# Attention keys transposed by DMA instead of by TensorE, with block-wide loads, a deeper MLP lag and an instruction order made from modelled times

## The chip, the cores and the metric

The kernel runs on one core of a Trainium2 chip. The metric is the device time of one execution in microseconds (us).

The engines are named as the profile names them. PE is TensorE (matmuls, and transposes done as matmuls), PEld is its weight load, DVE is VectorE, ACT is ScalarE, POOL is GpSimd. SP only issues DMAs here, on its own queue (SPq). The program fixes the order of the instructions on each engine. In the traces of this case an instruction that waits holds up those behind it on its engine (below, DVE stands 11.6 us before one instruction while others are behind it), and this whole case turns on that.

## The reference, cut to what matters

B=4 batches, H=8 heads, S=768 tokens, D=64. Keys are grouped into 24 chunks of 32. An upper bound of each query's score against a chunk comes from the chunk's elementwise minimum and maximum. Each query attends only to its six best chunks, causally. The result is fed to a two-layer ELU network, 512 to 2048 to 512.

```python
k_min = np.min(k_chunks, axis=3); k_max = np.max(k_chunks, axis=3)   # over 32 keys
ub = np.sum(np.maximum(q * k_min, q * k_max), axis=-1)               # bound of query x chunk
top_chunks = np.argsort(np.where(causal, ub, -1e9))[..., -6:]
attn = softmax(where(selected and causal, q @ k.T / 8, -1e9)) @ v    # shortened
h = x @ w_in
out = np.where(h > 0, h, np.exp(np.minimum(h, 0)) - 1) @ w_out
```

## The kernel before

The work is cut into eight blocks, one for each batch and half of the queries. In a block, for each pair of heads, K and Q are transposed on PE, the bounds are computed, chunks are selected, and scores, exponentials and PV follow. The normalised attention of a block then goes through the MLP: 64 matmuls `h_ps` (128x384) and 48 matmuls `o_ps` (128x512) for each block, so 512 and 384 in the whole run.

Attention has many small steps that wait for one another across PE, ACT and DVE. MLP matmuls have few such waits. So the kernel tells the scheduler, by priorities (`span`), to run the MLP of block i among the attention of block i+1, as filler for PE.

```python
def prep(t, hf):                              # one pair of heads
    ...
    for n in range(3):
        nc.tensor.transpose(ps[:, P * n:P * (n + 1)], k_pair[:, n], ident_f)    # psK
    nc.vector.tensor_reduce(out=kmm[:, 0, :], in_=pv, axis=AX.X, op=AOT.min)    # chunk bounds
    nc.vector.tensor_reduce(out=kmm[:, 1, :], in_=pv, axis=AX.X, op=AOT.max)
    for h in range(2):
        nc.scalar.activation(out=lhs[s][h][0:64, ts], in_=ps[64 * h:64 * h + 64, :], func=AF.Copy)
    ...                                       # rows 64 to 95 of lhs: constant mask rows
for i in range(len(blocks)):
    at = span(i, *SP_A[i])
    for t in pairs_of(blocks[i][0]):
        attend(t, blocks[i][1], ...)
    mm_h, last_e = mlp(*blocks[i], span(i + 1, *SP_M[i]))   # SP_M = [(0.0, 1.0)] * 8
    ...                                       # loads, front (prep and select) of block i + 1
```

The names in the profile: `psK`, `psQ` and `pxt` are transposes done on PE, `ub` the bounds, `sps` the scores, `pt` their exponentials, `o` the products with V, `on` the normalised attention and `xt` its transpose. `lhs` and `rhs` hold the transposed keys and queries.

In `mlp`, each `h_ps` tile goes through ACT (exp), POOL (minus one) and DVE (`gT`, the ELU). It occupies one of four PSUM buffers until the DVE step has read it.

The softmax here doesn't subtract the row's maximum and nothing guards it: scores larger than these inputs give would overflow.

## Time and profile before

| | before |
|---|---|
| median of 3 runs | 338.99 us (338.86 to 339.16) |
| span of the profiled run | 338.3 us |
| PE busy, idle | 303.8, 34.5 us |
| ACT, DVE, POOL busy | 231.4, 223.2, 98.3 us |
| DMA queue q1 (SP's: most loads of Q, K and V, transposes, stores), share of 16 engines | 32.8% |

Here are lines of the page of the kernel before: the busy time of the engines, then busy tenths in 40 equal slices of the span. PEclk is the granted TensorE clock in tenths.

```profile
PE 303.8 (90%) x2328; PEld 165.8 (49%) x2328; DVE 223.2 (66%) x690; ACT 231.4 (68%) x506; POOL 98.3 (29%) x219
...
PE   3776999998899979999989998999999998999895
...
PEclk9955799999999998999999999999999999999999
DMA  7899977542422677566232313223200111000001
```

After the fifth slice (about 42 us) PE is at nine tenths nearly everywhere, while DMA falls well below full. These are the groups of instructions that matter, with busy us, mean ns of one, and the idle time just before them with what ended most of it:

```profile
L321 PE MATMUL h_ps<-xt,w_in_sb 128*128 128x384 bf16 x512 | 107.1, 334 | 8.3 <-DMA xt<-on 4.6
L334 PE MATMUL o_ps<-w_out_sb,gT 128*128 128x512 bf16 x384 | 99.5, 379 | 0.9 <-DVE gT L328 0.8
...
L179 PE MATMUL psK<-ident_f,k_pair 128*128 128x128 f32 x96 | 20.0, 300 | 6.1 <-POOL kst_146 L138 4.1
L181 DVE TENSOR_REDUCE kmm<-psK 128x12 f32<-128x384 f32 x32 | 17.6, 550 | 6.3 <-PE psK L179 6.1
```

PE's waits in the kernel before (total us, times, longest us) are all small:

```profile
PE h_ps L321 <- DMA xt<-on: 4.6, 5, 2.3
PE psK L179 <- POOL kst_146 L138: 4.1, 1, 4.1
PE pxt L306 <- DVE on L299: 3.7, 3, 1.4
PE h_ps L321 <- DVE gT L328: 3.5, 8, 1.0
```

The windows view of the kernel before, 60 to 140 us. Columns: stretch and its length, then busy us with the count of instructions for PE, PEld, DVE, ACT and POOL, then the granted clock, the DMA share and GB/s.

```profile
60.00:80.00 20.00, 18.87 (x168) 9.70 (x166) 12.71 (x51) 17.65 (x40) 0.00 (x0) 1.00 0.48 122
80.00:100.00 20.00, 17.07 (x155) 10.03 (x155) 15.75 (x50) 18.60 (x42) 4.97 (x10) 1.00 0.33 73
100.00:120.00 20.00, 18.77 (x157) 9.48 (x156) 15.95 (x55) 12.32 (x26) 7.36 (x15) 1.00 0.44 103
120.00:140.00 20.00, 17.22 (x115) 9.52 (x113) 13.05 (x40) 13.14 (x31) 8.07 (x17) 0.91 0.69 166
```

### The profile page before, as it was taken

The numbers are of one execution on the slowest core, as the hardware profiler recorded it, in microseconds if no ns is written. First come the engines' busy times: TensorE is split into PE (matmuls) and PEld (weight loads), VectorE is DVE, ScalarE is ACT, GpSimd is POOL, SyncE is SP. The second block draws the span as 40 slices with busy tenths as digits, with TensorE's granted clock in tenths as the row PEclk, the third lists the DMA queues.
The fourth block names the chain that finished last, engine by engine and source line by source line (L and its number), as shares of the span: only waits on it lengthen the run. The fifth ranks groups of instructions, "written<-read, shape, count | busy, mean of one in ns | idle before, by whom it ended". The sixth has DMA issues, their size and how long they took to land.

```text
span 338.3 us, 6875 instructions
## 1 busy us (share of the span) xinstructions
PE 303.8 (90%) x2328; PEld 165.8 (49%) x2328; DVE 223.2 (66%) x690; ACT 231.4 (68%) x506; POOL 98.3 (29%) x219
## 2 busy tenths in 40 slices
PE   3776999998899979999989998999999998999895
PEld 2444544444454435555654455555554445545552
DVE  5888578566798673875479874866479765622640
ACT  5643585799995718976797649966797647856531
POOL 8750442000055214641153003420053004400530
PEclk9955799999999998999999999999999999999999
DMA  7899977542422677566232313223200111000001
GB/s 175 163 186 202 200 161 175 155 114 60 103 51 60 137 179 186 133 140 148 71 87 52 98 56 89 61 58 92 75 14 12 45 39 37 0 33 34 31 24 69
DMA packets 94498, 32.16 MB, mean 95 GB/s; under 512 B 87296, under 2 KB 91392, under 8 KB 94464
## 3 DMA queue, kind: packets, MB, share of 16 engines
q1 hardware_dynamic: 88640, 27.15, 32.8%
q0 software_dynamic: 4224, 4.19, 7.6%
q10 hardware_dynamic: 1600, 0.39, 0.5%
q8 instruction: 18, 0.29, 0.4%
q14 instruction: 16, 0.13, 0.1%
HBM read 27.26 MB, written 6.29 MB: 99 GB/s over the span
## 4 chain that ended last, share of the span: by engine, by line
PE 32%; DVE 24%; issue 18%; ACT 17%; POOL 5%; DMA 3%; SPq 0%; POOLq 0%; ACTq 0%
PE o_ps L334 11%; PE h_ps L321 9%; DVE gT L328 6%; ACT pt L265 5%; ACT e_sb L325 4%; PE sps L262 4%; PE ub L220 3%; POOL e_sb L326 3%; DMA xt<-on 2%; DVE kmm L181 2%; DVE kmm L182 2%; PE psK L179 1%; DVE on L299 1%; DVE ubT L223 1%; DMA v_pair<-in_v_dram 1%
## 5 line engine op out<-in xcount | busy, mean ns | idle before, releaser
L326 POOL TENSOR_SCALAR e_sb<-e_sb 128x384 f32<-128x384 f32 x128 | 65.7, 521 | 190.8 <-ACT e_sb L325 186.9
L321 PE MATMUL h_ps<-xt,w_in_sb 128*128 128x384 bf16 x512 | 107.1, 334 | 8.3 <-DMA xt<-on 4.6
L334 PE MATMUL o_ps<-w_out_sb,gT 128*128 128x512 bf16 x384 | 99.5, 379 | 0.9 <-DVE gT L328 0.8
L328 DVE SCALAR_TENSOR_TENSOR gT<-h_ps,e_sb 128x384 bf16<-128x384 f32 x128 | 69.1, 552 | 32.7 <-POOL e_sb L326 30.9
L265 ACT ACTIVATE pt<-sps 128x384 bf16<-128x384 f32 (+1 forms) x160 | 79.0, 538 | 16.6 <-PE sps L262 15.3
L325 ACT ACTIVATE e_sb<-h_ps 128x384 f32<-128x384 f32 x128 | 61.3, 502 | 30.5 <-PE h_ps L321 29.9
L321 PEld LDWEIGHTS <-w_in_sb 128*128 128x128 bf16 x512 | 49.6, 100 | 40.8 <-issue 17.2
L334 PEld LDWEIGHTS <-gT 128*128 128x128 bf16 x384 | 35.4, 97 | 36.5 <-issue 3.8
L337 ACT ACTIVATE o_sb<-o_ps 128x512 f32<-128x512 f32 x24 | 14.3, 598 | 35.4 <-PE o_ps L334 32.2
L293 PEld LDWEIGHTS <-pt 128*128 128x128 bf16 x672 | 29.2, 100 | 17.6 <-DVE pt L274 5.1
L274 DVE TENSOR_TENSOR pt<-pt,tri_196 128x512 bf16<-128x512 bf16 x32 | 14.3, 446 | 18.8 <-ACT pt L265 18.8
L179 PE MATMUL psK<-ident_f,k_pair 128*128 128x128 f32 x96 | 20.0, 300 | 6.1 <-POOL kst_146 L138 4.1
L181 DVE TENSOR_REDUCE kmm<-psK 128x12 f32<-128x384 f32 x32 | 17.6, 550 | 6.3 <-PE psK L179 6.1
L268 ACT ACTIVATE pt<-sps 128x512 bf16<-128x512 f32 x32 | 19.5, 609 | 2.6 <-PE sps L262 2.2
L199 ACT ACTIVATE QTf<-psQ 128x192 f32<-128x192 f32 (+1 forms) x32 | 13.2, 413 | 10.1 <-PE psQ L198 7.0
L198 PE MATMUL psQ<-ident_f,q_pair 128*128 128x128 f32 x96 | 18.3, 304 | 1.2 <-ACT lhs_155 L184 0.3
L202 DVE TENSOR_SCALAR Qrl<-QTf 128x192 f32<-128x192 f32 (+1 forms) x32 | 11.7, 365 | 11.5 <-ACT QTf L199 11.0
L179 PEld LDWEIGHTS psK<-ident_f,k_pair 128*128 128x128 f32 x96 | 12.0, 149 | 13.0 <-POOL kst_146 L138 4.1
L182 DVE TENSOR_REDUCE kmm<-psK 128x12 f32<-128x384 f32 x32 | 17.5, 547 | 0.0
L198 PEld LDWEIGHTS psQ<-ident_f,q_pair 128*128 128x128 f32 x96 | 11.3, 151 | 11.8 <-ACT lhs_155 L184 2.0
L280 DVE TENSOR_TENSOR pt<-pt,tri_196 128x256 bf16<-128x256 bf16 x32 | 10.6, 333 | 7.7 <-ACT pt L268 7.7
L223 DVE STREAM_TRANSPOSE ubT<-ub 128x192 f32<-128x192 f32 (+1 forms) x16 | 7.7, 480 | 11.3 <-PE ub L220 11.3
(348 smaller groups left out, 400.7 us busy)
## 6 DMA issues: line engine op xcount, KB each, us to landing
k_pair<-in_k_dram SPq DMA_DIRECT2D x64, 96.0 KB, 2.5
v_pair<-in_v_dram SPq DMA_DIRECT2D x64, 96.0 KB, 2.4
out_dram<-o_sb SPq DMA_DIRECT2D x24, 256.0 KB, 2.1
q_pair<-in_q_dram SPq DMA_DIRECT2D x60, 96.0 KB, 2.4
w_in_sb<-in_moe_w_in_dram POOLq DMA_DIRECT2D x4, 512.0 KB, 8.4
w_out_sb<-in_moe_w_out_dram POOLq DMA_DIRECT2D x4, 512.0 KB, 17.0
q_pair<-in_q_dram ACTq DMA_DIRECT2D x4, 96.0 KB, 2.9
xt<-on SPq DMA_TRANSPOSE x24, 2.4
```

What stands on the lines that cost most here:

```text
L179: nc.tensor.transpose(ps[:, P * n:P * (n + 1)], k_pair[:, n], ident_f)
L181: nc.vector.tensor_reduce(out=kmm[:, 0, :], in_=pv, axis=AX.X, op=AOT.min)
L182: nc.vector.tensor_reduce(out=kmm[:, 1, :], in_=pv, axis=AX.X, op=AOT.max)
L198: nc.tensor.transpose(ps[:, P * n:P * (n + 1)], q_pair[:, n], ident_f)
L265: nc.scalar.activation(out=pt[:, hd, 0:wtot], in_=sps[:, 0:wtot], func=AF.Exp, scale=SCALE)
L268: nc.scalar.activation(out=pt[:, :, 0:256], in_=sps[:, :].rearrange("p (h w) -> p h w", h=2), func=AF.Exp, scale=SCALE)
L293: nc.tensor.matmul(o3[:, hd, qi, :], lhsT=pt[:, hd, P * qt + off:P * qt + off + P], rhs=vexts[s][:, kb, hd, :], start=(kb == 0), stop=(kb ...
L321: mm = nc.tensor.matmul(hw, lhsT=w_in_sb[:, kk, P * fc:P * (fc + 1)], rhs=xT[NPAIR * b + kk, hf], start=(kk == 0), stop=(kk == NKK - 1))
L325: nc.scalar.activation(out=e_sb, in_=hw, func=AF.Exp)
L326: last_e = nc.gpsimd.tensor_scalar(out=e_sb, in0=e_sb, scalar1=-1.0, scalar2=1.0, op0=AOT.add, op1=AOT.mult)
L328: nc.vector.scalar_tensor_tensor(out=gT[:, fc, :], in0=hw, scalar=0.0, in1=e_sb, op0=AOT.max, op1=AOT.min)
L334: nc.tensor.matmul(o_ps, lhsT=gT[:, fc, P * tt:P * (tt + 1)], rhs=w_out_sb[:, fc, :], start=(fc == 0), stop=(fc == NFC - 1))
```

## The change

Its intent is to relieve PE. K is cast to bf16 on POOL into padded tiles that already hold the mask rows, and the DMA engines transpose them. Only block 0 keeps its K on PE. The chunk bounds come from a second copy of K, loaded chunk by chunk into 96 partitions and reduced there by DVE. Loads are block-wide, and the MLP lags two blocks more. One line asks the scheduler to order the instructions by a simulated timeline, that is, by modelled times. I call this "the modelled order". The core of the diff, with cuts marked:

```diff
-SP_A = [(0.0, 0.5)] + [(0.0, 0.9)] * 7
-SP_F = [(0.5, 1.0)] + [(0.0, 0.8)] * 7
+SP_A = (0.0, 0.9)
+SP_F = (0.0, 0.8)
+LAG = 3
 ...
+    ctx.enter_context(tc.block(schedule_with_timeline_sim=True))
 ...
+    def load_c(b, hf):                      # K again, one chunk of 32 keys in each partition
+        kc = ldpool.tile([H * HCH, CHUNK * D], F32, name="kc", bufs=1)
 ...
+    def bounds(b, hf, behind=()):
 ...
+        kv = kc[:, :].rearrange("p (w d) -> p d w", d=D)
+        for x in range(2):
+            for w, op in ((0, AOT.min), (1, AOT.max)):
+                d2 = slice(D // 2 * x, D // 2 * (x + 1))
+                red = nc.vector.tensor_reduce(out=kmm[:, w, d2], in_=kv[:, d2], axis=AX.X, op=op)
 ...
+        nc.tensor.transpose(kT[:, 0:n], kmm[...], ident_f[0:n, 0:n])
 ...
+    def keys(b, hf):
 ...
+        for n in range(3):
+            casts += [nc.gpsimd.tensor_scalar(out=kbn[hf][:, n, :, 0:D], in0=kl[:, n], ...)]
+            nc.sync.dma_start_transpose(out=lh[:, n], in_=kbn[hf][:, n].rearrange("p h d -> p (h d)"))
 ...
-    casts = vpart(0)
-    w_ins = []
-    with tc.issue_after(casts[1].ins):
-        w_ins += [load_w_in(0), load_w_in(1)]
+    vpart(0)
+    load_block(1)
 ...
+    casts = back(1, (-0.3, 0.0))            # back: bounds and keys of a block
+    with tc.issue_after(casts[WGATE].ins):
+        w_ins = [load_w_in(i) for i in range(4)]
 ...
-        mm_h, last_e = mlp(*blocks[i], span(i + 1, *SP_M[i]))
+        mm_h, last_e = mlp(*blocks[i], span(i + LAG, *SP_M))
 ...
+            back(i + 2, SP_B, [norms[j] for j in BEHIND])
```

## The prediction

> **What bounds the kernel now.** TensorE. The page gives PE 303.8 of 338.3 us busy (90%), ACT 231 (68%), DVE 223 (66%), POOL 98 (29%). After 40 us the twenty-microsecond windows leave PE idle only 0.4 to 2.9 us each, so what shortens PE's work shortens the kernel. The Trainium skill, "Perfetto Trace Analysis", section Identifying the Most-Contended Engine, warns that matmul busy time is not distance to the roofline. The trace agrees: in the pure MLP tail the chain shows 48 h_ps matmuls in 7.96 us (166 ns each) and 48 o_ps in 10.37 us (216 ns), while over the whole run the groups give 209 and 259 ns of busy time each. From such dense pieces I estimate PE's real work at about 283 us: MLP 168, scores 36, PV 20, K and Q transposes 18 each, bounds 19, pxt 3. So some 55 us of the span are start, a low granted clock (0.5 from 17 to 34 us), small waits (26 us listed for PE: xt transposes 4.6, gT 4.3, on 3.7, ...), and loss from interleaving.
>
> **Removed.** 84 of 96 K transposes on PE: 3 take 0.55 us in a dense stretch, so 15.4 us of PE (17.5 us by busy time). 56 K evictions on ACT, 0.48 us each: about 27 us. On DVE 56 reduces of 0.55 us (31 us), 56 small tensor_tensors of 0.2 us (11 us), most of the mask-row copies (about 6 us).
>
> **Added.** 28 DVE reduces of 96x1024 elements: estimated 1.1 to 1.3 us each from 384 elements in 0.55 us, 31 to 36 us, so no gain there; small copies, 3 us. DVE falls by about 10 us in all. POOL: 21 K casts of 512 columns, est. 0.7 us each from 0.52 us for 384, 15 us; it has room. 21 DMA transposes of eight 128x128 blocks: the three-block one takes 1.18 us to issue and 2.4 us to land, so est. 3 us and 4 to 5 us; SP's queue has room and they are prefetched a block ahead. Another 5.5 MB of K is read in long rows; DMA is only full before 45 us.
>
> **Moved.** MLP lags two blocks and is always ready filler, and the order is made from modelled times: xt, gT and on waits (about 12 us) should mostly vanish. But block 1's four loads (3.1 MB at about 180 GB/s, 17 us) come before or among the weights, so the first h_ps should move from 32.6 to 37-45 us, with attention of blocks 0 and 1 filling PE thinly, and perhaps a longer low-clock stretch. The tail is a long dense MLP.
>
> **Sum.** Before, at 42 us about 262 of the 283 us of work remained and took 294 us (89%). After, about 248 remain at 42 us; at 89% that is 278 us, end 320; at 93%, end 309. I take 313 us, range 301 to 327. Chances: faster by over 2% 0.90, within 2% 0.07, slower 0.03.
>
> **What would show it.** PE busy 275 to 292 us; ACT near 205; DVE 205 to 220; POOL 105 to 120; psK only 12 transposes; first h_ps at 37-45 us; busy time per h_ps matmul below 200 ns; no xt entry over 2 us in PE's waits. Wrong if: h_ps start later than 50 us; a granted clock near 0.5 beyond 45 us; PE waiting on DMA transposes (scores on lhs); DVE's 1.2 us reduces blocking gT and so PE over 8 us in all; the modelled order fitting the chip badly, with head-of-line waits on PE or SP.
>
> **What would make it wrong.** Chiefly a weak start (little PE work before weights land), or strided reduces slower than one element per cycle, making DVE the limit.

## The result, and the profile after

The kernel after took 366.12 us (median of four runs, 365.93 to 366.73), against 338.93 us for the kernel before in the same rounds. The ratio is 1.081, with a 95% interval of 1.079 to 1.083: slower, where I had given slower three chances in a hundred. All ratios here are the mean time of one kernel's runs over that of the other's runs in the same rounds, so they are not quite the ratio of the medians quoted. Executions over 1.5% slower than the fastest of the same kernel are left out of the means.

| | before | after |
|---|---|---|
| span | 338.3 | 364.1 |
| PE busy | 303.8 | 297.3 |
| PE idle (span less busy) | 34.5 | 66.8 |
| of it up to 40 us | 12.0 | 16.6 |
| 40 to 80 us | 2.4 | 18.7 |
| 80 to 200 us | 9.5 | 20.2 |
| after 200 us | 10.6 | 11.2 |
| ACT, DVE, POOL busy | 231.4, 223.2, 98.3 | 207.8, 239.9, 111.7 |
| share of DMA queue q1 | 32.8% | 60.1% |

Set beside before, the loss lies in PE standing idle between 40 and 200 us (27 us more) and a little before that. Here are the same lines of the page of the kernel after:

```profile
PE 297.3 (82%) x2235; PEld 164.8 (45%) x2251; DVE 239.9 (66%) x629; ACT 207.8 (57%) x450; POOL 111.7 (31%) x220
...
PE   4756575349676877999968999999899999998795
...
PEclk9955988559989896999996999999999999999899
DMA  8899999999899899999998470020421002010002
```

DMA is full for more than half of the span, where it had been only at the start. The groups after (the trace misses 16 of the 384 `o_ps` records, worth about 16 x 0.24 = 4 us, so PE's true busy time is up to 301 us):

```profile
L400 PE MATMUL h_ps<-xt,w_in_sb 128*128 128x384 bf16 x512 | 104.9, 342 | 20.1 <-DVE gT L407 19.5
...
L413 PE MATMUL o_ps<-w_out_sb,gT 128*128 128x512 bf16 x368 | 88.3, 385 | 1.5 <-DVE gT L407 0.5
...
L204 DVE TENSOR_REDUCE kcm<-kc 96x32 f32<-96x1024 f32 x28 | 51.5, 1888 | 14.9 <-DMA kc<-in_k_dram 11.6
```

PE's waits after:

```profile
PE h_ps L400 <- DVE gT L407: 19.5, 8, 10.0
PE pxt L382 <- DVE on L375: 7.0, 4, 5.4
...
PE sps L337 <- DMA lhs_369<-kbn_140: 4.0, 1, 4.0
```

The wait for `xt`, which the lag was to remove, is gone. In its place PE waits 19.5 us for `gT`, that is, for DVE, ten of them at once. It also waits 4.0 us for keys transposed by DMA (`lhs`), a sign that the prediction had named. The windows view after shows where (same columns as before):

```profile
60.00:80.00 20.00, 7.90 (x26) 3.18 (x27) 10.01 (x13) 6.92 (x14) 2.59 (x5) 0.51 1.13 162
80.00:100.00 20.00, 17.16 (x149) 9.39 (x149) 6.88 (x17) 9.27 (x21) 5.70 (x10) 0.98 0.97 186
100.00:120.00 20.00, 14.83 (x165) 9.22 (x166) 18.20 (x56) 13.42 (x29) 4.72 (x8) 0.91 1.15 204
120.00:140.00 20.00, 13.30 (x89) 5.87 (x87) 16.30 (x47) 14.48 (x32) 4.46 (x8) 0.88 1.08 164
```

From 60 to 80 us PE ran 26 matmuls instead of 168, at about half the clock. The Trainium skill, "TensorE: Matmul & The Clock Gate", section Part 1: The HAM clock gate, says that a PE which idles for a window of a few microseconds drops to half clock until it has been busy again. The trace agrees on the drop: PE was idle from 57.1 to 61.1 us, in the wait for `lhs`, and the granted clock fell to 0.5 at 60.3 us. It stayed there until 80.8 us, also from 62 to 68 us, where PE was busy for 4.8 of 6 us.

The causes of this stall can be followed through three timelines. Columns: start us, us, engine or queue, line, operation, output and input, count; in brackets the idle time before it and what ended that. First, the queue of SP in the kernel after:

```profile
28.95 27.19 SPq L226 DMA_TRANSPOSE lhs_369<-kbn_140  x3
56.24 5.13 SPq L109 DMA_DIRECT2D kc<-in_k_dram  x8
```

Issuing three transposes of keys holds the queue for 27 us, while the weights are being loaded. Only then can the loads of `kc` for the next block be issued. Second, DVE:

```profile
69.99 7.19 DVE L204 TENSOR_REDUCE kcm<-kc 96x32 f32<-96x1024 f32 x4 [11.61 <-DMA kc<-in_k_dram]
77.10 1.47 DVE L407 SCALAR_TENSOR_TENSOR gT<-h_ps,e_sb 128x384 bf16<-128x384 f32 x3
```

DVE stands 11.6 us at the reduces because `kc` has not landed. The reduces take 7.2 us, and only behind them in DVE's order come the `gT` steps that free PSUM. Third, PE:

```profile
77.70 1.44 PE L400 MATMUL h_ps<-xt,w_in_sb 128*128 128x384 bf16 x4 [9.99 <-DVE gT L407]
```

So one late DMA passed through DVE's order and then through PE's order, and cost PE 10 us. That explains this stall, but not yet the 27 us of the result, as the experiments show.

Why 256-byte packets were slow there can be counted in the trace. From 29 to 56 us, while the three transposes were being issued, 3767 packets of 256 bytes of SP's queue moved beside 3862 packets of 1024 bytes of the weights, about one for one. The Trainium skill, "DMA: Bandwidth & Descriptors", section Queues, rings and completion order, states that an engine takes turns between its queues packet by packet. The trace agrees in so far as the two counts are nearly equal. It does not show how many of the packets that it lists go in one turn. So the small packets got a fifth of the bytes (3767 x 256 over the sum of both).

A second difference is less visible: how evenly the MLP is spread. The table counts `h_ps` and `o_ps` matmuls started in each stretch, from the windows view of these tiles.

| us | 60-80 | 80-100 | 100-120 | 120-140 | 140-160 | 160-180 | 180-200 |
|---|---|---|---|---|---|---|---|
| before | 28 | 36 | 55 | 57 | 54 | 69 | 58 |
| after | 7 | 53 | 11 | 11 | 64 | 67 | 36 |

### The profile page after: what moved, and what is told of

Its sections match the earlier page's. It is cut to its first block, busy times and chain, and to the rows that moved or that the text cites. A ratio compares the mean times of both kernels' runs of the same rounds, so it can differ in the third digit from the quotient of the medians.

```text
span 364.1 us, 6429 instructions
## 1 busy us (share of the span) xinstructions
PE 297.3 (82%) x2235; PEld 164.8 (45%) x2251; DVE 239.9 (66%) x629; ACT 207.8 (57%) x450; POOL 111.7 (31%) x220
## 3 DMA queue, kind: packets, MB, share of 16 engines
q1 hardware_dynamic: 110480, 38.16, 60.1%
## 4 chain that ended last, share of the span: by engine, by line
PE 52%; DMA 19%; DVE 16%; ACT 4%; SPq 3%; issue 2%; POOL 2%; DVEq 0%; ACTq 0%
PE o_ps L413 20%; PE h_ps L400 17%; DVE kcm L204 7%; DMA kc<-in_k_dram 5%; DMA v_ld<-in_v_dram 5%; PE sps L337 5%; PE ub L294 4%; DMA lhs_369<-kbn_140 4%; DMA k_ld<-in_k_dram 3%; DVE gT L407 2%; SPq L102 2%; DVE on L375 1%; POOL e_sb L405 1%; ACT pt L341 1%; PE psQ L272 1%
## 5 line engine op out<-in xcount | busy, mean ns | idle before, releaser
L400 PE MATMUL h_ps<-xt,w_in_sb 128*128 128x384 bf16 x512 | 104.9, 342 | 20.1 <-DVE gT L407 19.5
L341 ACT ACTIVATE pt<-sps 128x384 bf16<-128x384 f32 (+1 forms) x160 | 81.2, 533 | 44.7 <-PE sps L337 44.1
L413 PE MATMUL o_ps<-w_out_sb,gT 128*128 128x512 bf16 x368 | 88.3, 385 | 1.5 <-DVE gT L407 0.5
L204 DVE TENSOR_REDUCE kcm<-kc 96x32 f32<-96x1024 f32 x28 | 51.5, 1888 | 14.9 <-DMA kc<-in_k_dram 11.6
L413 PEld LDWEIGHTS <-gT 128*128 128x128 bf16 x384 | 37.1, 99 | 44.0 <-issue 4.4
L369 PEld LDWEIGHTS <-pt 128*128 128x128 bf16 x672 | 31.1, 102 | 20.3 <-DVE pt L350 6.6
L272 PE MATMUL psQ<-ident_f,q_ld 128*128 128x128 f32 x96 | 19.0, 311 | 2.7 <-ACT rhs_135 L275 1.1
L224 POOL TENSOR_SCALAR kbn_140<-k_ld 128x512 bf16<-128x512 f32 x12 | 7.4, 618 | 32.4 <-DMA k_ld<-in_k_dram 26.1
L272 PEld LDWEIGHTS psQ<-ident_f,q_ld 128*128 128x128 f32 x96 | 13.1, 159 | 7.2 <-ACT rhs_135 L275 1.5
L356 DVE TENSOR_TENSOR pt<-pt,tri_154 128x256 bf16<-128x256 bf16 x32 | 10.1, 315 | 7.6 <-ACT pt L344 7.6
L188 POOL TENSOR_SCALAR vext_127<-v_ld 128x512 bf16<-128x512 f32 (+1 forms) x13 | 8.0, 619 | 19.2 <-DMA v_ld<-in_v_dram 19.2
L224 POOL TENSOR_SCALAR kbn_139<-k_ld 128x512 bf16<-128x512 f32 x9 | 5.7, 630 | 21.3 <-DMA k_ld<-in_k_dram 21.2
```

Source lines behind the costliest of these rows:

```text
L204: red = nc.vector.tensor_reduce(out=kmm[:, w, d2], in_=kv[:, d2], axis=AX.X, op=op)
L272: nc.tensor.transpose(ps[:, P * n:P * (n + 1)], ql[:, n, 2 * r:2 * r + 2], ident_f)
L341: nc.scalar.activation(out=pt[:, hd, 0:wtot], in_=sps[:, 0:wtot], func=AF.Exp, scale=SCALE)
L369: nc.tensor.matmul(o3[:, hd, qi, :], lhsT=pt[:, hd, P * qt + off:P * qt + off + P], rhs=vexts[b % 2][:, kb, 2 * r + hd, :], start=(kb == 0 ...
L400: mm = nc.tensor.matmul(hw, lhsT=w_in_sb[:, kk, P * fc:P * (fc + 1)], rhs=xT[NPAIR * b + kk, hf], start=(kk == 0), stop=(kk == NKK - 1))
L413: nc.tensor.matmul(o_ps, lhsT=gTs[fc // 4][:, fc % 4, P * tt:P * (tt + 1)], rhs=w_out_sb[:, fc, :], start=(fc == 0), stop=(fc == NFC - 1))
```

## The experiments

My first theories were these. A: the start, where block 1's loads, transposes and the weights collide. B: the new path of K itself, above all the strided reduces and their bursts on DVE. The rivals were that the modelled order (theory C in the expectations) or the lag (theory D) fits the chip badly whatever is done with K. "Wrong" marks kernels that give a wrong result by design.

| run | one-line description | median us | ratio to before |
|---|---|---|---|
| e_wfirst | after, weights first | 371.73 | 1.092 |
| e_kpe | e_wfirst, K of all blocks on PE | 365.67 | 1.080 |
| e_notsim | after, no modelled order | 413.74 | 1.221 |
| e_lag1 | after, LAG 1 | 378.86 | 1.120 |
| e_before_tsim | before + modelled order | 364.63 | 1.077 |
| e_kpe_lag1 | e_kpe, LAG 1 | 361.38 | 1.069 |
| e_kpe_notsim | e_kpe, no modelled order | 352.43 | 1.042 |
| e_kpe_lag1_notsim | both | 348.55 | 1.031 |
| n_kpe | the last, with the start order of before | 345.85 | 1.021 |
| n_kdma | n_kpe with K by DMA | 433.58 | 1.281 |
| n_kdma2 | n_kdma, other priorities of the bounds | 434.23 | 1.281 |
| e_contig | after, contiguous reduces (wrong) | 362.86 | 1.072 |
| e_clump | before, MLP gathered by priorities | 354.84 | 1.049 |
| n_knone | n_kpe, K work in blocks 0 and 1 only (wrong) | 331.71 | 0.980 |
| n_ktr | n_knone + K loads, casts, DMA transposes (wrong) | 341.85 | 1.010 |
| n_kdma3 | n_kdma, bounds earlier, more buffers | 401.88 | 1.184 |
| n_kdma3s | n_kdma3, reduces of 2 rows in 32 (wrong) | 376.65 | 1.112 |
| b_bal15 | before, MLP spread otherwise | 344.78 | 1.020 |

### First batch: which part of the change?

**e_wfirst**: the weights are loaded as early as before, and block 1's loads wait for them.

```diff
-    vpart(0)
-    load_block(1)
-    ...
-    with tc.issue_after(casts[WGATE].ins):
-        w_ins = [load_w_in(i) for i in range(4)]
+    casts = vpart(0)
+    w_ins = []
+    with tc.issue_after(casts[1].ins):
+        w_ins += [load_w_in(0), load_w_in(1)]
+    ...
+    for d in load_block(1):
+        tc.add_manual_dep(d.ins, w_ins[GATE].ins.name, SYNC, reason="order")
```

> The changed kernel (366 us) with the weights issued as early as in the kernel before (behind the first casts of V) and block 1's loads held until the last piece of w_in has landed, so that they and block 1's K transposes no longer share the DMA with the weights. Theory A (the loss is made in the first 80 us, where weights and block 1's K transposes collide on the DMA engines and SP's queue sits 27 us on three transposes): 343 to 352 us, the three transposes issue in under 8 us in all, PE busy by 80 us up from 45 to over 55 us. Theory B (the DMA and DVE cost of the K path all along the first 200 us): under 5 us gained, 361 to 366. Theory C (the order fixed from modelled times): unpredictable, within 8 us of 366.

It took 371.73 us, no faster than the kernel after. That is in the range of theory C. Yet the transposes no longer collided with the weights. This is the queue of SP in this run:

```profile
54.12 4.50 SPq L226 DMA_TRANSPOSE lhs<-kbn  x2
...
59.32 1.23 SPq L226 DMA_TRANSPOSE lhs<-kbn  x1
```

Issuing three transposes now takes 5.7 us and not 27. PE's idle time from 40 to 80 us was still 20.0 us, and from 80 to 200 us it rose from 20.2 to 28.1. But only the first link of the stall was taken away. `kc` was still late, as DVE's timeline shows:

```profile
70.83 7.22 DVE L204 TENSOR_REDUCE kcm<-kc 96x32 f32<-96x1024 f32 x4 [9.55 <-DMA kc<-in_k_dram]
```

Behind these reduces PE waited 11.5 us, now at a transpose of queries. So theory A falls as it was put: the collision with the weights is not what makes the loss. A late `kc` and the burst of reduces are not ruled out by this run.

**e_kpe**: e_wfirst with K on PE in every block (`OWN = tuple(range(8))`, no `bounds` and `keys`). The lag, the loads and the modelled order stay.

> As the run with early weights, and K for every block goes the way of block 0: transposed on PE, bounds reduced from PSUM, mask rows written once; no second K load, no padded tiles, no K transposes by DMA. Lag of two blocks, block-wide loads and the modelled order stay. Theory B (K path): at or below the kernel before, 325 to 340 us, with DMA share well under 1 after 80 us. Theory A (start alone): the same as the run with early weights plus some 10 us for the PE transposes that come back. Theory C (modelled order or lag at fault): still over 350 us.

It took 365.67 us, 6 us less than e_wfirst. The intervals of the two ratios overlap (1.073 to 1.086, and 1.082 to 1.102), so this difference is not clear of the noise. Moving K back to PE adds 8.7 us of PE busy time (298.2 to 306.9) and takes 14.7 us of idle time away (71.6 to 56.9; both traces miss 15 or 16 PE records). 27 us of loss against before are left with K on PE. So theory B alone falls too, going by the total.

The place of the idle time says more than the total. From 40 to 200 us PE is idle for 48.0 us in e_wfirst and for 19.5 us in e_kpe. The stall behind `kc` does go away with the new path of K. But e_kpe is idle for 18.7 us before 40 us and 18.7 us after 200 us, where e_wfirst has 12.3 and 11.4. The modelled order is another one there. So the equal totals do not show that the kernel after and e_kpe lose their time in the same way.

**e_notsim**: after without the one line that asks for the modelled order.

```diff
-    ctx.enter_context(tc.block(schedule_with_timeline_sim=True))
```

> The changed kernel with the order from modelled times switched off; everything else stays, the order then follows the priorities as in the kernel before. Theory C (modelled order misfits the chip): 340 us or less. Theories A and B: 360 us or more, since the same transfers collide.

It took 413.74 us, 48 us slower. For the kernel with K by DMA the modelled order is a help: by priorities alone its MLP stands in clumps, with stretches of 3, 17, 0 and 20 MLP matmuls in 20 us, and others of 63, 75 and 78. The 3 and 17 are those of 100 to 140 us, where the kernel after has 11 and 11, so the modelled order is not what thins the filler there.

**e_lag1**: after with `LAG = 1`.

> The changed kernel with the MLP's place in the order moved up by two slots, to where the kernel before had it (the slot after its attention). Theory D (lag: MLP work is held back while PE waits for the DMA-bound attention): 345 us or less, with more o_ps matmuls before 100 us. Theories A and B: within 6 us of 366.

It took 378.86 us, 12.7 us slower. The lag helps the kernel after, as predicted, but it does not pay for the rest.

### Second batch: the modelled order on the kernel before

**e_before_tsim**: before, with only this line added.

```diff
+    ctx.enter_context(tc.block(schedule_with_timeline_sim=True))
     warm = const.tile([P, 1], F32, name="warm")
```

> The kernel before with one line added: the order comes from modelled times. K by PE and the runs with K by PE and with the modelled order switched off have left theories A and B short: K back on PE did not bring the time back (366 us), switching off the modelled order made it worse (414). If the modelled order by itself misfits the chip (theory C): 350 us or more. If it is harmless: 330 to 343 us, and lag or the block-wide loads are at fault.

It took 364.63 us against 338.48 for before, ratio 1.077 (1.073 to 1.080): 26 us slower. All instructions and loads are those of before; only the order differs. This is the central finding of the experiments. PE's largest waits in this run:

```profile
PE h_ps L322 <- DVE gT L329: 9.1, 13, 1.6
PE ub L221 <- DVE kmm L187: 6.9, 1, 6.9
```

The waits are spread over many places. No single stall is large enough, and PE's idle time is 55.6 us against 34.5. Of the 21 us more, 5.7 lie before 40 us, 2.7 from 40 to 80, 5.0 from 80 to 200 and 7.7 after that. The windows view for the tile `h_ps` (PE busy, count, granted clock, DMA share, GB/s) shows the thinnest stretch, first in before, then in e_before_tsim:

```profile
60.00:80.00 20.00, 1.95 (x8) 1.00 0.48 122
80.00:100.00 20.00, 7.00 (x36) 1.00 0.33 73
```

```profile
60.00:80.00 20.00, 0.81 (x4) 0.83 0.38 101
80.00:100.00 20.00, 2.23 (x8) 0.66 0.31 70
```

With `o_ps` counted too, from 60 us on before has 28, 36, 55, 57 MLP matmuls in 20 us, and e_before_tsim has 13, 8, 45, 62. Attention ran with little filler from 60 to 100 us, PE idled 7.1 us against 4.1 in before, in waits that were all under 1 us, and the granted clock fell to 0.66. DMA was no busier than in before in these stretches, so full DMA engines are not the reason. The clock can explain only a small part of the 26 us: over the whole span its mean is 0.953 against 0.964, which makes 34 us at half clock instead of 24, so at most 5 us of work (an estimate from these numbers). Later stretches are uneven too: from 220 to 280 us e_before_tsim has 65, 53 and 37 MLP matmuls, before has 55, 66 and 63.

**e_kpe_lag1, e_kpe_notsim, e_kpe_lag1_notsim**: e_kpe with `LAG = 1`, without the modelled order, and with both edits.

> The run with K on PE (366 us), with the MLP's place in the order moved back up by two slots, as in the kernel before. Theory D (the lag costs): 345 us or less. If the modelled order or the block-wide loads cost: 358 us or more.

> The run with K on PE (366 us), with the order from priorities, lag of two blocks kept. Theory C: 345 us or less. If lag costs (theory D), 375 us or more, since by priorities alone the MLP is then held back behind everything.

> The run with K on PE (366 us), with neither lag nor modelled order: of the change only the block-wide loads, their single buffers and the shared tiles of keys and queries are left. If the lag and the modelled order are the whole loss: 336 to 345 us. If the block-wide loads cost: over 350 us, with SP waiting to refill a single buffer and PE waiting for transposes of K and Q.

The four kernels with K on PE make a square: with the modelled order 365.67 (LAG 3) and 361.38 (LAG 1), without it 352.43 and 348.55. The modelled order costs 13 us at either lag. The longer lag costs 4 us in either order. The two costs simply add. The two runs without the modelled order met none of the ranges expected; both lie between them. With K on PE, then, both parts of "Moved" that I had counted as gains are losses.

### Third batch: the rest of the way back to before, and K by DMA alone

**n_kpe**: e_kpe_lag1_notsim with the start order of before (`SP_A`, `SP_F`, the gate of the front of block 1, the order of the V casts).

> Of the change only the block-wide loads and shared tiles are left: K on PE, order from priorities, the MLP in the slot after its attention, and, unlike the earlier run of this kind (348.6 us), also the start of the kernel before: half a slot each for block 0's attention and block 1's front, and that front held behind the sixth MLP group. If that start was the rest of the difference: 334 to 342 us, level with the kernel before. If the block-wide loads themselves cost: 345 us or more.

It took 345.85 us, ratio 1.021 (1.016 to 1.025). What is left of the change here costs about 7 us: the block-wide loads with their single shared buffers, issued two blocks ahead, and with them larger tiles shared by the heads, `gT` in quarters with five buffers and 11 instead of 9 `pt` tiles. The wait that grew is this one (before had 0.2 us of it), as PE's waits of n_kpe show:

```profile
PE psK L242 <- DMA k_ld<-in_k_dram: 10.9, 5, 4.4
```

One buffer for a whole block of K can only be refilled when its last reader is done, so the next block's K arrives late. That reading is argued from this wait; no run tried a second buffer, and none took these parts singly.

**n_kdma and n_kdma2**: n_kpe with K by DMA; then the reduces given an earlier priority and the transpose of the bounds a later one.

> As n_kpe, but K for blocks 1 to 7 goes by the second K load, the padded tiles and the DMA transposes, as in the change. The difference to n_kpe is the K path alone, under the order of the kernel before. If the K path is worth what PE saves (15 us of transposes): 320 to 328 us. If its DMA and DVE cost eat it up: 340 us or more, with PE waiting for the bounds' transpose behind the 1.9 us reduces.

> As n_kdma, with the reduces of the bounds placed half a slot earlier in the order and their PE transpose only at the slot's end, so that PE should no longer sit behind DVE's reduces. If the waits of PE on the bounds are what n_kdma lacks: 5 to 15 us faster than n_kdma. If DMA capacity is: within 3 us of it.

They took 433.58 and 434.23 us. PE waited 29.2 us at `kT`, the transpose of the bounds, for `kcm` on DVE in n_kdma, and 28.8 us in n_kdma2: my change of priorities moved nothing. The waits lie behind the reduces on DVE, up to 8.5 us at once. The MLP was in clumps again (75, 0, 0, 3, 9, 68, 35, 13, 96 matmuls in successive 20 us). So this pair is not a clean measure of K by DMA. It only shows again that the order decides.

**e_contig**: after, with the reduces reading 32 neighbouring floats instead of 32 floats 64 apart (wrong: relative error 0.52).

```diff
-        kv = kc[:, :].rearrange("p (w d) -> p d w", d=D)
+        kv = kc[:, :].rearrange("p (d w) -> p d w", d=D)
```

> The changed kernel with the bounds' reduces reading each row's 2048 elements in order instead of with a step of 64; wrong bounds, so a wrong result on purpose; the instruction order on PE is the same as in the changed kernel. If the step costs: one reduce takes 1.1 to 1.2 us instead of 1.89, DVE 20 us less busy, and the time falls if DVE's reduces gate PE (355 to 362 us). If the step costs nothing: 1.85 to 1.95 us each and no change.

It took 362.86 us, 3 us less than after, just above the expected range. DVE fell to 222.0 us of busy time from 239.9. The group of the reduces in this run:

```profile
L204 DVE TENSOR_REDUCE kcm<-kc 96x32 f32<-96x1024 f32 x28 | 32.4, 1206 | 24.3 <-DMA kc<-in_k_dram 23.8 <-issue 0.6
```

One reduce takes 1.206 us contiguous and 1.888 us strided. The Trainium skill says as much in words: in "SBUF — State Buffer", section Door 1: The DMA port swizzle, the note on SBUF cachelines tells that fp32 elements further apart than a few lose read efficiency. The trace agrees, by a factor of 1.57. I had not looked it up when predicting. The contiguous duration fits the 1.1 to 1.3 us that I had estimated. The stride alone is worth little here; DVE then waits longer for `kc` (23.8 us instead of 11.6).

### Fourth batch: clumps without modelled order, and K by DMA in an even order

**e_clump**: before, with the MLP's priorities squeezed into the last third of a block.

```diff
-SP_M = [(0.0, 1.0)] * 8
+SP_M = [(0.0, 1.0)] + [(0.7, 1.0)] * 7
```

> The kernel before, order from priorities, with one number changed: the MLP of blocks 1 to 7 is placed in the last three tenths of its slot instead of spread over it. Counted per 100 matmuls of PE's program order, the MLP's share then scatters by 18 (standard deviation over the middle of the kernel) as with the modelled order (19), against 8 in the kernel before. If clumps are what the modelled order costs: 352 to 368 us. If they are harmless and something else of that order costs: 336 to 344 us.

It took 354.84 us, 16 us slower. From 140 us on its MLP counts are 35, 74, 29, 74, 39, 75, 30, where before has 54, 69, 58, 61, 55, 66, 63. So gathering the MLP costs 16 us by itself, with nothing modelled and nothing moved to DMA. It is a deliberate imitation of the uneven order, not a replica: its added idle time lies almost all between 80 and 200 us (8.4 us), and its PE busy time rises by 6.3 us, where that of e_before_tsim rises by 1.1. So it shows what an order about as uneven can cost. That 16 of the 26 us of e_before_tsim come from clumps is not shown.

**n_knone and n_ktr**: both are wrong. n_knone does no K work after blocks 0 and 1 and reuses their keys and bounds, so it shows the most that freeing PE of K can bring. n_ktr adds the K loads, the casts and the DMA transposes again, still without bounds. The counts of MLP matmuls per hundred PE instructions are nearly the same in the two traces, so the order is held.

```diff
# n_kpe to n_knone
-OWN = tuple(range(8))
+OWN = (0, 1)
-lhsT=ksts[(t // NPAIR) % 2][...]
+lhsT=ksts[0][...]
 ...                      # also: keys of blocks 0 and 1 for all, no K loads after them
# n_knone to n_ktr
 ...                      # also: K loads and two sets of keys again
-        return []
+        return keys(*blocks[i])
```

> As n_kpe (345.9 us), but the keys and bounds of blocks 0 and 1 are used for all later blocks: no K load, transposes, evictions or reduces in blocks 2 to 7; a wrong result on purpose. It is the ceiling of what any other K path can gain there. PE loses 72 transposes (13 us in dense stretches), ACT 23 us, DVE some 35 us. If PE's work sets the time: 329 to 335 us. If the gain cannot be had because PE waits for other things: over 340 us.

> As n_knone, with only the K loads, the casts into the padded tiles and the DMA transposes of blocks 2 to 7 added; the bounds still stale, wrong on purpose. If the DMA transposes cost little by themselves: within 4 us of n_knone, and the rest of the K path (bounds) is what eats the gain. If their DMA time or SP's queue costs: 8 us or more above n_knone.

n_knone took 331.71 us, 14.1 us below n_kpe. n_ktr took 341.85 us: the loads and transposes take 10.1 of those 14.1 us back. Part of both numbers is the plain loading of K, which n_knone drops and every right kernel needs. The cleaner comparison is n_ktr with n_kpe: 4.0 us less, still without bounds. The windows view (columns as before) from 60 to 150 us, n_knone first:

```profile
60.00:100.00 40.00, 36.79 (x323) 19.68 (x326) 23.25 (x84) 33.64 (x76) 2.69 (x6) 0.96 0.33 75
100.00:150.00 50.00, 46.71 (x360) 25.61 (x362) 34.24 (x102) 31.23 (x73) 21.34 (x39) 1.00 0.54 107
```

```profile
60.00:100.00 40.00, 35.32 (x318) 18.12 (x319) 23.86 (x82) 33.26 (x75) 5.91 (x10) 1.00 1.04 185
100.00:150.00 50.00, 45.00 (x356) 25.11 (x356) 36.01 (x105) 31.09 (x73) 26.32 (x49) 1.00 0.86 171
```

DMA goes from a third to full (60 to 100 us), and PE loses a little everywhere, as at `xt` (6.3 us of waits in n_ktr, 1.4 in n_knone). So the transposes do not come free even where PE's order is even. The bounds are still to be paid out of the 4 us that remain.

**n_kdma3**: n_kdma with the bounds' priority much earlier (`SP_B = (-0.7, -0.6)`), `kT` in the PSUM pool of the MLP, two buffers of keys, and nine `pt` tiles.

> The whole K path by DMA as in n_kdma (433.6 us), correct result, with the bounds placed half a slot earlier, their PE transpose in the MLP's PSUM pool and the key tiles double-buffered: the MLP's share per 100 matmuls then scatters by 15 instead of 27. If clumps and PE waiting for the bounds are what n_kdma lost: 345 to 375 us. If the DMA traffic of the K path is: over 400 us still.

It took 401.88 us. PE's longest wait, 23.1 us, is at the first transpose of bounds. DVE's timeline and then PE's show it:

```profile
43.16 7.20 DVE L207 TENSOR_REDUCE kcm<-kc 96x32 f32<-96x1024 f32 x4 [15.40 <-DMA kc<-in_k_dram]
```

```profile
50.67 0.42 PE L212 MATMUL kT<-ident_f,kcm 96*128 96x96 f32 x1 [23.14 <-DVE kcm L210]
```

So 15.4 us of it is `kc` of block 1, whose loads wait for the weights in this kernel, and 7.2 us is the burst of reduces. Later bursts cost PE less at once: the one at 158 us held it for 3.6 us.

### Fifth batch: the bursts, and an attempt to beat both

**n_kdma3s**: n_kdma3 with reduces over 2 of 32 rows (wrong), with almost the same order on PE.

```diff
-in_=kv[:, d2], axis=AX.X, op=op)
+in_=kv[:, d2, 0:2], axis=AX.X, op=op)
```

> As n_kdma3 (401.9 us), but each reduce of the bounds reads only 2 of the 32 rows of its chunk: wrong bounds, so wrong on purpose, and DVE's burst per block falls from 7.2 us to under 1 us. The order on PE past the start is the same. If DVE's bursts are what the K path loses: 345 to 360 us. If the order (attention gathered, MLP gathered) and the DMA traffic lose it: 385 us or more.

It took 376.65 us, 25 us below n_kdma3 and between the two ranges expected, with reduces of 0.206 us instead of 1.88. So of the 60 us that lie between n_ktr and n_kdma3, the length of the reduces makes 25. A wait at `kT` remains with short reduces (19.3 us in all, 18.0 of it in one wait that ends at 44.4 us), and DVE stands 16.8 us at them for `kc`. The start holds a part of the other 35 us: up to 60 us PE is busy for 30.5 us here and for 40.3 us in n_ktr. How the rest divides between the order and the traffic of `kc` I could not separate.

**b_bal15**: before, with the MLP of every second block reaching into the next.

```diff
-SP_M = [(0.0, 1.0)] * 8
+SP_M = [(0.0, 1.15), (0.15, 1.0)] * 4
```

> The kernel before with the MLP moved a little from the slots with heavy attention (second halves of a sequence) into those with light attention: it starts 0.15 slot later after a second half and ends 0.15 slot later after a first half. If evenness of ACT's load beside the MLP still leaves something: 333 to 337 us. If the kernel before is at its best: 337 to 342 us.

It took 344.78 us, ratio 1.020, worse than both ranges expected. No kernel with a right result beat the kernel before.

### What the steps add up to

Each step changes one thing or one group of things. The medians come from different chips and rounds; before stayed between 338.2 and 339.1 in all of them. The last two steps are not clear of the noise.

| step | us | difference |
|---|---|---|
| before | 338.9 | |
| n_kpe: block-wide loads, shared tiles, buffers | 345.9 | +7 |
| e_kpe_lag1_notsim: start order | 348.6 | +3 |
| e_kpe_notsim: longer lag | 352.4 | +4 |
| e_kpe: modelled order | 365.7 | +13 |
| e_wfirst: K by DMA | 371.7 | +6 |
| after: weights later | 366.1 | -6 |

The steps are not independent of their sequence. The modelled order costs 26 us on before and 13 on e_kpe, and it gains 48 us on after.

## Why the prediction was wrong

**The step that failed** is this one, as the prediction put it: "MLP lags two blocks and is always ready filler, and the order is made from modelled times: xt, gT and on waits (about 12 us) should mostly vanish." From it came the efficiency of 93%, end 309, and it was the only ground for going beyond 89%. Not even the 89% held: the 248 us of work that I had left at 42 us took 322 us, which is 77%, and PE's idle time after 42 us rose from 22.3 to 50.1 us. In its place the runs showed that the modelled order costs 26 us when it is added to before alone, and 13 us on the kernel with K on PE, where the longer lag costs 4 us. Filler that is ready does not help if the order does not put it there. The kernel after has 11 and 11 MLP matmuls in 100 to 140 us, where before had 55 and 57. The `xt` wait did vanish; the `gT` wait went from 3.5 to 19.5 us and `on` from 3.7 to 7.0. The prediction named this risk ("the modelled order fitting the chip badly, with head-of-line waits") but gave it next to no weight.

This does not make the modelled order the cause of the loss in the kernel after: there it is worth 48 us against the order by priorities. With K by DMA both orders leave PE short of filler from 100 to 140 us (11 and 11 MLP matmuls, or 3 and 17), and why is open. What the traces do show there is the path that the prediction took to be free: a late `kc`, then 7.2 us of reduces on DVE, then 10.0 us in which PE waited for `gT`. The prediction had set "over 8 us in all" for such a wait as a sign that it was wrong.

**The saving on PE had the right size, but it came with costs that were left out.** I counted 15.4 us for the K transposes of seven blocks. With all K work of six blocks gone, n_knone gained 14.1. Its PE busy time fell by 11.9 us, of which up to 4 may be records missing from its trace. Work on ACT, DVE and DMA went away too, so the nearness of 14.1 to 15.4 is partly luck. And K by DMA also takes DMA capacity: n_ktr gives 10.1 us back, the plain loads of K included. I had written that DMA "is only full before 45 us". In the kernel after, the share in the windows view is 0.9 to 1.3 in every 20 us up to 200 us (the view adds up packet times, so it can pass 1), against 0.3 to 0.7 in before from 60 to 140 us.

**The transposes by DMA** I estimated at 3 us to issue and 4 to 5 to land. In n_ktr they land in 3.4 us (median), and free of the weights three take 5.7 us to issue. So the estimate was somewhat high, and not what failed. What I missed is the first three, which held the queue for 27 us beside the weight load and so delayed `kc`. Yet undoing this (e_wfirst) gained nothing, as `kc` came no earlier.

**The reduces** I sized at 1.1 to 1.3 us; they took 1.888, because of the stride. That made 51.5 us on DVE where I had 31 to 36. So DVE came to 239.9 and not to 205 to 220: it rose by 17 us where I had it fall by 10. The Trainium skill, "VectorE: DVE Perf Modes", section The perf-mode tier table, lists only the slowest mode (1x) for a tensor reduce. The traces fit this, though no run tries another mode: 1.206 us for 1024 contiguous elements is 1.2 ns each, against 0.550/384 = 1.4 ns in the kernel before (read from PSUM), so the longer reduce is hardly faster. I had that rate, but not the stride. Four of them in a row also hold DVE for 7.2 us, while `gT` and `pt` wait behind. In n_kdma3 the length of the reduces is worth 25 us; in the kernel after only the stride was tested (e_contig, 3 us).

**What came out as predicted**: the first `h_ps` at 40.3 us (37 to 45), ACT 207.8 (near 205), POOL 111.7 (105 to 120), psK only 12, no `xt` wait over 2 us. **What did not**: PE busy 297.3 (275 to 292), and busy time of an `h_ps` matmul 104.9/512 = 205 ns, not below 200, so PE was hardly denser than before (209). The caution from the Trainium skill, "Perfetto Trace Analysis", section Identifying the Most-Contended Engine, held: busy time was not the work, for PE's fell by 2.5 to 6.5 us (depending on the missing records) while the kernel lost 27. The sign "a granted clock near 0.5 beyond 45 us" showed too, at 60 to 80 us.

**What stays open.** How much of the 26 us that the modelled order costs on before comes from clumps is not shown; an imitation (e_clump) costs 16. Nor is it shown how the 27 us of the result divide between the order, the lag and the new path of K, since each of these changes what the others cost. I also do not know which of the modelled durations is wrong; no run here shows the model's times. Why priorities alone clump the MLP as soon as K goes by DMA (e_notsim, n_kdma) is not shown. The 35 us of n_kdma3s over n_ktr are not fully divided between start, order and the loads of `kc`. And that the block-wide loads make the 7 us of n_kpe is read from one wait, not tested.

## What to carry to other kernels

If a change brings an automatic order with it, measure that one line on the old kernel and on the new one: here a single line cost 26 us on the one and gained 48 us on the other, and it hid behind three larger parts that looked more important. Work taken from the busiest engine is a gain only if what replaces it neither fills a resource that engine waits for (here DMA: 10 of 14 us, plain loads included) nor stands in a long burst ahead of its releases in another engine's order (here 7.2 us on DVE). Count the filler matmuls per stretch of time, not only the busy shares; two totals that look alike can hide an even order and a clumped one.

## What the Trainium skill lacked or had wrong

- "SBUF — State Buffer": it names the loss of strided fp32 reads but gives no size for a reduce. Here a step of 64 floats made a reduce of 96x1024 elements 1.888 us instead of 1.206, 1.57 times as long.
- "DMA: Bandwidth & Descriptors": it has the turns between queues, but not what they do to a queue of small packets beside one of large packets. Here three transposes held the issuing queue for 27.2 us beside the weight load, against 5.7 us without it, and 256-byte packets got about a fifth of the bytes.
- "DMA: Bandwidth & Descriptors", section Latency and other measured facts, gives an effective 261 GB/s for DMA transposes. Another page has the time of one 128x128 block alone; none has one for eight blocks in one transpose within SBUF. Eight 128x128 bf16 blocks are 262 KB, so about 1.0 us at that rate (an estimate); here they landed 3.4 us after their issue (median of 18, n_ktr).
- No page tells how an order made from modelled times compares with one made by priorities. Here it was 26 us slower on the kernel before and 48 us faster on the kernel after.
